# Storing the rows of x from SyncE's queue in place of GpSimd's, in an attention and two-stage expert kernel

## The chip, the cores and the metric

The kernel runs on one core of a Trainium2 chip. The metric is device time in microseconds. A core has five engines with instruction queues of their own: TensorE (PE; PEld is its weight load), VectorE (DVE), ScalarE (ACT), GpSimd (POOL) and SyncE (SP), which only issues transfers here. Transfers run on 16 DMA engines that all issuers share. Each engine takes its instructions strictly in order; waits between engines, and for transfers to land, are semaphores.

## The reference

Three stages follow one another: block attention, a layer of experts with one expert per token, and a second dense layer with a maximum of three products.

```python
# attention: B, H, S, D = 8, 8, 576, 64, in chunks of 64 keys
scores = scale * np.matmul(q_c, k_c.transpose(0, 1, 2, 4, 3))
attn = np.exp(scores - np.max(scores, axis=-1, keepdims=True))
attn = attn / (np.sum(attn, axis=-1, keepdims=True) + 1e-09)
out = np.matmul(attn, v_c)
x = out.transpose(0, 2, 1, 3).reshape(B * S, H * D)        # 4608 tokens x 512
# experts: a token with x @ w_skip > 0 goes to expert argmax(x @ w_gate)
h = np.maximum(xc[mask] @ w1[e], 0.0)                       # 512 -> 1024
y[mask] = gate_w[mask, None] * (h @ w2[e])                  # 1024 -> 512
out[do_compute] = xc + y
# second layer
h = np.maximum(np.maximum(x @ w1, x @ w2), x @ w3)          # 512 -> 768
return h @ w_out
```

## The kernel before

The 4608 tokens are 36 tiles of 128. A loop over t = 0 to 35 runs the attention as a pipeline: in step t the scores of tile t, the values and the scaling of tile t - 2, the transpose of x of that tile, and the logits of tile t - 3. Four tiles make a group g (nine groups). The rows of x of a group lie in one buffer `xg` of 128 partitions x 4 tiles x 520 floats; there are two such buffers, so group g + 2 writes where group g was. `scaled(t)` writes a tile's rows (L361, VectorE); at a group's first tile a memset on GpSimd fills the padding columns first (L357). `route(g)` and `gates(g)` choose the experts on VectorE; `gates(g)` writes one gate value per row (L432) and then calls `store_x(g)`, the function of this study, which copies the buffer to `x_dram`. Later the experts' rows are gathered from `x_dram` by indirect transfers on GpSimd.

GpSimd has further work in this loop: it copies halves of v across partitions (`cross`, L259), pairs the heads of q and k (`pair_heads`, `pair_big`, L233), rounds expert weights (L771), and sends each token's number to its slot in a table in DRAM (`send_id`, L524). SyncE loads q and k (L213, L222, L226), v (L252), expert weights (L100, L763), and reads the table of slots back (L540), once the sends have landed. Its loads of q, k and v run up to eight tiles ahead of their use.

What sets the order: on PE, DVE, ACT and POOL the program's order inside `by_hand` is kept as it is written. On SyncE a scheduler with a timeline of its own decides it. Every transfer of a queue takes one of eight semaphores in turn (DMAHW0 to 7 for SyncE), and waits until the one that had it before has landed.

```python
parts = [bpool.tile([P, GT, XW], F32, tag="xg", name=f"xg{g}")]   # two buffers
...
nc.vector.reciprocal(part[:, :, DM], sm[:, i * n:i * n + n])
store_x(g)
```

Of the kernel before, what the change touches and what calls it, by code (L numbers as in the profile page):

```python
# [19 lines left out]
P = 128  # L20
# [20 lines left out]
def kernel(  # L41
# [15 lines left out]
    nc = tc.nc  # L57
# [5 lines left out]
    x_dram = dram.tile([N + 1, XW], F32, name="x_dram")  # L63
# [356 lines left out]
    def gates(g):  # L420
        parts, nt = groups[g][0], SIZES[g]
        T = slice(0, nt)
        ex, m8, comp = routing[g]
        oh, eo = picks[g]
        sm = apool.tile([P, GT], F32, tag="rsm", name=f"rsm_{g}", bufs=1)
        nc.vector.reduce_sum(sm[:, T], ex[:, T], axis=AX)
        nc.vector.tensor_scalar(eo[:, T], m8[:, T], float(-COLS), float(E * COLS + P * SLOTS), op0=ALU.mult, op1=ALU.add)
        nc.vector.tensor_scalar_add(sm[:, T], sm[:, T], 1e-9)
        nc.vector.scalar_tensor_tensor(eo[:, T], comp[:, T], float(-P * SLOTS), eo[:, T], op0=ALU.mult, op1=ALU.add)
        for i, part in enumerate(parts):  # L430
            n = part.shape[1]
            nc.vector.reciprocal(part[:, :, DM], sm[:, i * n:i * n + n])  # L432
        store_x(g)
        before, after = run[g % 2], run[(g + 1) % 2]
        got = apool.tile([P, E], F32, tag="rgot", name=f"rgot_{g}", bufs=1)
        nc.vector.reduce_sum(got, oh[:, T].rearrange("p t e -> p e t"), axis=AX)
        nc.vector.tensor_tensor(after, before, got, op=ALU.add)
# [104 lines left out]
    def store_x(g):  # L542
        r = START[g] * P
        for part in groups[g][0]:
            n = part.shape[1] * P
            nc.gpsimd.dma_start(x_dram[r:r + n, :].rearrange("(t p) c -> p t c", p=P), part)
            r += n

    def apart(ins, own, other):
# [785 lines left out]
    for b, (r0, n) in enumerate(BLOCKS):  # L1335
# [31 lines left out]
        for half in range(2):  # L1367
            for i in range(n // P):
# [11 lines left out]
                r = r0 + half * n + i * P  # L1380
# [34 lines left out]
```

## Time and profile before

| | |
|---|---|
| median of three timed runs | 1050.54 us (1046.76 to 1053.8) |
| the profiled execution | 1043.47 us |
| its span in the trace | 1041.8 us |
| TensorE busy | 999.0 us |
| VectorE busy | 575.4 us |
| ScalarE busy | 420.2 us |
| GpSimd busy | 315.6 us |
| the nine stores of x | 1040.0 KB each |

All times inside the trace count from the start of the span. The span is one profiled execution, some 1.7 us shorter than the time of that execution, and that execution was a little faster than the timed ones. "Idle before" is the time in which an engine did nothing before an instruction, with what ended it; a row of SyncE is the issuing of a transfer, not the transfer.

### The profile page before, as it was taken

Reading aid. Unit: us, or ns where it says so; the run is one execution under the profiler, and the core shown is the slowest. Engines: PE = TensorE matmul, PEld = TensorE weight load, DVE = VectorE, ACT = ScalarE, POOL = GpSimd, SP = SyncE. Lnnn points to the kernel's source line nnn. Section 1 sums busy time; section 2 is a strip of 40 time slices with the busy share of each in tenths; the row PEclk is TensorE's granted clock in tenths of the full one; section 3 lists DMA queues with packets and bytes.
Section 4 is the critical chain, followed back from the end, with each engine's and each line's share of the span. In section 5 each row is a group of like instructions: output and inputs, shape, how many; then the busy total and the mean of one; then the engine's idle time right before and its main releaser. Section 6 shows DMA issues by size and latency. Waiting matters only on the chain.

```text
span 1041.8 us, 19679 instructions
## 1 busy us (share of the span) xinstructions
PE 999.0 (96%) x7569; PEld 855.2 (82%) x7569; DVE 575.4 (55%) x1100; ACT 420.2 (40%) x762; POOL 315.6 (30%) x359
## 2 busy tenths in 40 slices
PE   8998999998989999899999999999999999999996
PEld 7988988888777888787878887788888888878995
DVE  4676888688273795655898524343344424434241
ACT  5876874455251554424443422223222322223230
POOL 3665867512120343105321502213012311103010
PEclk9998999999999999999999999999999999999999
DMA  9999973877281795659995446645566356674771
GB/s 235 295 307 293 238 237 111 260 248 272 87 284 62 250 329 200 234 188 349 339 319 169 149 142 185 192 132 172 162 193 190 103 168 200 185 222 156 224 232 40
DMA packets 198258, 217.44 MB, mean 209 GB/s; under 512 B 47195, under 2 KB 162027, under 8 KB 198144
## 3 DMA queue, kind: packets, MB, share of 16 engines
q1 hardware_dynamic: 185328, 176.27, 55.7%
q0 software_dynamic: 10224, 31.40, 8.7%
q10 hardware_dynamic: 2592, 8.26, 2.1%
q8 instruction: 70, 1.15, 0.5%
q14 instruction: 44, 0.36, 0.1%
HBM read 175.30 MB, written 41.98 MB: 209 GB/s over the span
## 4 chain that ended last, share of the span: by engine, by line
PE 51%; DMA 3%; DVE 2%; issue 0%; ACT 0%; SPq 0%; DVEq 0%; ACTq 0%
PE f_a L663 6%; PE f_a L665 6%; PE f_a L664 6%; PE o L663 5%; PE o L665 5%; PE o L664 5%; PE f_d L663 3%; PE f_d L665 3%; PE f_d L664 3%; DMA ws<-m_sums 2%; PE f_b L663 2%; PE f_b L665 2%; PE f_b L664 2%; PE trf L1124 1%; DMA x<-x_dram 1%; PE h L663 0%
## 5 line engine op out<-in xcount | busy, mean ns | idle before, releaser
L94 POOL TENSOR_TENSOR fh<-best,fh 128x512 fp32r<-128x512 f32 (+1 forms) x60 | 75.2, 1260 | 358.1 <-ACT fh L93 271.1
L663 PE MATMUL f_a<-x_t,ws 128*128 128x512 f32 (+1 forms) x270 | 100.3, 372 | 0.8 <-DVE best L1298 0.8
L665 PE MATMUL f_a<-x_t,ws 128*128 128x512 f32 (+1 forms) x270 | 99.6, 369 | 0.0
L664 PE MATMUL f_a<-x_t,ws 128*128 128x512 f32 (+1 forms) x270 | 99.5, 369 | 0.0
L664 PE MATMUL o<-wlo_m,fh 128*128 128x512 f32 x216 | 84.6, 392 | 0.0
L663 PE MATMUL o<-whi_m,fh 128*128 128x512 f32 x216 | 84.5, 392 | 0.0
L665 PE MATMUL o<-whi_m,fh 128*128 128x512 f32 x216 | 83.4, 393 | 0.0
L943 POOL DMA_INDIRECT x_dram<-xg,ids_sb x20 | 30.0, 1501 | 172.5 <-DVE xg L941 81.0
L93 ACT CAST whi_e<-raw_e 128x1024 fp32r<-128x1024 f32 x56 | 58.2, 1051 | 58.8 <-DMA raw_e<-in_moe_w_dram 39.0
L663 PE MATMUL h<-xhi,whi_e 128*128 128x256 f32 x256 | 73.5, 287 | 7.9 <-PEq L1240 2.8
L94 DVE TENSOR_TENSOR wlo_e<-raw_e,whi_e 128x1024 fp32r<-128x1024 f32 x56 | 68.0, 1222 | 20.6 <-ACT whi_e L93 20.2
L663 PE MATMUL y<-whi_e,hhi 128*128 128x512 f32 x184 | 74.0, 403 | 0.9 <-ACT hhi L1012 0.9
L93 ACT CAST fh<-best 128x512 fp32r<-128x512 f32 (+1 forms) x60 | 34.5, 579 | 95.0 <-DVE best L1300 58.3
L664 PE MATMUL h<-xlo,whi_e 128*128 128x256 f32 x256 | 72.5, 283 | 0.2 <-issue 0.2
L665 PE MATMUL y<-whi_e,hlo 128*128 128x512 f32 x184 | 72.5, 397 | 0.2
L665 PE MATMUL h<-xhi,wlo_e 128*128 128x256 f32 x256 | 72.5, 283 | 0.0
L664 PE MATMUL y<-wlo_e,hhi 128*128 128x512 f32 x184 | 72.2, 393 | 0.0
L1130 POOL TENSOR_TENSOR x_t<-t,x_t 128x512 fp32r<-128x512 f32 (+1 forms) x40 | 46.1, 1182 | 50.9 <-ACT x_t L1129 50.9
L1303 ACT COPY p<-f_a 128x512 f32<-128x512 f32 (+1 forms) x45 | 24.3, 543 | 87.0 <-PE f_a L665 86.8
L663 PEld LDWEIGHTS f_a<-x_t,ws 128*128 128x128 f32 x270 | 51.0, 189 | 9.9 <-DVE best L1298 1.6
L665 PEld LDWEIGHTS f_a<-x_t,ws 128*128 128x128 f32 x270 | 50.9, 189 | 8.6
L663 PEld LDWEIGHTS h<-xhi,whi_e 128*128 128x128 f32 x256 | 49.2, 192 | 10.7 <-issue 9.3
(242 smaller groups left out, 2604.8 us busy)
## 6 DMA issues: line engine op xcount, KB each, us to landing
ws<-m_sums SPq DMA_DIRECT2D x135, 512.0 KB
raw_e<-in_moe_w_dram SPq DMA_DIRECT2D x64, 512.0 KB
ws<-m_sums SPq DMA_DIRECT2D x45, 256.0 KB
x_dram<-xg POOLq DMA_DIRECT2D x9, 1040.0 KB, 6.5
x<-x_dram SPq DMA_DIRECT2D x36, 256.0 KB
v_all<-in_v_dram SPq DMA_DIRECT2D x32, 256.0 KB
out_dram<-os SPq DMA_DIRECT2D x32, 256.0 KB
m_sums<-n_raw ACTq DMA_DIRECT2D x18, 448.0 KB
```

The costliest lines, as they stand in the source:

```text
L93: nc.scalar.copy(hi, src),
L94: eng.tensor_tensor(lo, src, hi.bitcast(F32), op=ALU.subtract),
L663: nc.tensor.matmul(acc, ahi, bhi, start=first, stop=False, skip_group_check=onto)
L664: nc.tensor.matmul(acc, ahi, blo, start=False, stop=False, skip_group_check=onto)
L665: return nc.tensor.matmul(acc, alo, bhi, start=False, stop=last, skip_group_check=onto)
L943: ins = nc.gpsimd.indirect_dma_start(out=x_dram[:, :], out_offset=bass.IndirectOffsetOnAxis(ap=ids, axis=0), in_=xg, in_offset=None, bound ...
L1124: nc.tensor.transpose(tr[:, i * P:(i + 1) * P], row[:, c * P:(c + 1) * P], ident)
L1130: eng.tensor_tensor(lo, src, hi.bitcast(F32), op=ALU.subtract)
L1303: nc.scalar.copy(p1, acc_a)
```

## The change

A group's store is issued by SyncE and no longer by GpSimd. Size, source, destination and the work on the four computing engines stay.

```diff
     def store_x(g):
         r = START[g] * P
         for part in groups[g][0]:
             n = part.shape[1] * P
-            nc.gpsimd.dma_start(x_dram[r:r + n, :].rearrange("(t p) c -> p t c", p=P), part)
+            nc.sync.dma_start(x_dram[r:r + n, :].rearrange("(t p) c -> p t c", p=P), part)
             r += n
```

The order on PE, DVE and ACT is the same. On SyncE, at about t = 10 to 13 of the loop, the rows before were these; `qt` and `kt` are buffers of q and k, `v_all` of v, and in brackets is what a row waits for.

```order
L222 DMA qt_927<-in_q_dram 128x4x256 [waits DMAHW3_49,Pool_49]
L222 DMA kt_928<-in_k_dram 128x4x256 [waits DMAHW4_49,Pool_49]
L252 DMA v_all_139<-in_v_dram 128x8x64 [waits DMAHW5_49,PE_49,Activation_49]
L222 DMA qt_1121<-in_q_dram 128x4x256 [waits DMAHW6_49,Pool_49]
L222 DMA kt_1122<-in_k_dram 128x4x256 [waits DMAHW7_49,Pool_49]
L252 DMA v_all_140<-in_v_dram 128x8x64 [waits DMAHW0_49,PE_49,Activation_49]
L252 DMA v_all_141<-in_v_dram 128x8x64 [waits PE_49,DMAHW1_49,Activation_49,Pool_49]
```

Now, in the same place, with `xg_374`, the buffer of group 0:

```order
L222 DMA qt_927<-in_q_dram 128x4x256 [waits DMAHW3_49,Pool_49]
L222 DMA kt_928<-in_k_dram 128x4x256 [waits DMAHW4_49,Pool_49]
L252 DMA v_all_139<-in_v_dram 128x8x64 [waits DMAHW5_49,PE_49,Activation_49]
L546 DMA x_dram<-xg_374 128x4x520 [waits DMAHW6_49,DVE_49]
L222 DMA qt_1121<-in_q_dram 128x4x256 [waits DMAHW7_49,Pool_49]
L222 DMA kt_1122<-in_k_dram 128x4x256 [waits DMAHW0_49,Pool_49]
L252 DMA v_all_140<-in_v_dram 128x8x64 [waits DMAHW1_49,PE_49,Activation_49]
L252 DMA v_all_141<-in_v_dram 128x8x64 [waits PE_49,DMAHW2_49,Activation_49,Pool_49]
```

The store of group 0 stands between two loads and waits for VectorE's gates; the loads behind it wait until it is issued.

On VectorE the order is the same, and the rows around the first scaling of group 2 (`xg_1148`, the buffer that `xg_374` had) are now these; before, the same row waited for DMASW5, a semaphore of GpSimd's queue.

```order
L359 TENSOR_SCALAR sm_1151<-xp_1131 128x8 [waits PE_49]
L360 RECIPROCAL sm_1151<-sm_1151 128x8 [waits DVE_49]
L361 TENSOR_TENSOR xg_1148<-xp_1131,sm_1151 128x2x4x64 [waits DMAHW6_49,DVE_49,Pool_49]
L313 TENSOR_REDUCE mx_1173<-sc_1156 128x8 [waits PE_49]
L315 TENSOR_TENSOR ex_1175<-sc_1156,mx_1173 128x2x4x64 [waits DVE_49,Activation_49]
L401 TENSOR_REDUCE rmx_1204<-lg_735 128x4 [waits Activation_49]
```

The wait for the buffer goes from GpSimd's semaphore to SyncE's, and the maximum and the subtraction of the tile stand behind it.

On SyncE, near the end of the loop, the difference is this; `ids_121` and `ids_sb` are the slot lists, and 2776, 3181 and 3550 are the buffers of groups 6, 7 and 8.

```order
 L540 DMA ids_121<-ids_dram_67 128x3
 L540 DMA ids_sb<-ids_dram_67 128x288
+L546 DMA x_dram<-xg_2776 128x4x520
+L546 DMA x_dram<-xg_3181 128x4x520
 L540 DMA ids_120<-ids_dram_68 128x1
+L546 DMA x_dram<-xg_3550 128x4x520
 L616 DMA n_raw_4513<-in_moe_w_dram 128x2x512
 L616 DMA n_raw_4791<-in_moe_w_dram 128x2x512
```

The stores of groups 6 and 7 come behind two loads of slot lists that wait for GpSimd's sends, and that of group 8 behind a third.

## Rows read from the trace of the kernel before

**Rows 1.** The page: busy time of each engine, and the stores among the issues.

```profile
PE 999.0 (96%) x7569; PEld 855.2 (82%) x7569; DVE 575.4 (55%) x1100; ACT 420.2 (40%) x762; POOL 315.6 (30%) x359
...
x_dram<-xg POOLq DMA_DIRECT2D x9, 1040.0 KB, 6.5
```

**Rows 2.** Waits of TensorE, 40 to 190 us: total us, times, longest us.

```profile
PE sc L306 <- issue: 6.0, 4, 2.5
PE lp L385 <- ACT xt L379: 1.0, 1, 1.0
PE xp L345 <- issue: 0.9, 2, 0.5
PE lp L385 <- issue: 0.5, 1, 0.5
PE rk L458 <- DVE roh L415: 0.4, 1, 0.4
PE trx L374 <- DVE xg L361: 0.2, 1, 0.2
```

**Rows 3.** Stretches: us, PE, PEld, DVE, ACT, POOL busy, then PEclk, DMA share, GB/s.

```profile
40.00:56.00 16.00, 14.71 (x309) 13.92 (x309) 9.99 (x33) 11.55 (x26) 11.02 (x23) 1.00 1.03 300
56.00:70.00 14.00, 14.00 (x324) 13.17 (x324) 12.12 (x37) 11.79 (x27) 8.80 (x14) 1.00 1.09 312
...
92.00:99.00 7.00, 7.00 (x92) 6.55 (x90) 4.55 (x15) 3.58 (x9) 1.41 (x3) 0.51 1.02 247
99.00:103.00 4.00, 4.00 (x93) 3.84 (x93) 1.92 (x11) 2.94 (x8) 2.87 (x5) 1.00 0.70 216
```

**Rows 4.** Timeline of GpSimd: start, us, instruction, idle before and its releaser.

```profile
44.70 0.78 POOL L546 DMA_DIRECT2D x_dram<-xg  x1
...
55.13 0.12 POOL L357 MEMSET xg<- 128x28 f32 x1 [0.26 <-DMA x_dram<-xg]
...
62.44 0.82 POOL L546 DMA_DIRECT2D x_dram<-xg  x1 [3.93 <-DVE run L437]
...
148.83 0.81 POOL L546 DMA_DIRECT2D x_dram<-xg  x1 [4.77 <-DVE run L437]
```

**Rows 5.** Timeline of SyncE, 53 to 76 us.

```profile
57.56 1.06 SPq L252 DMA_DIRECT2D v_all<-in_v_dram  x1
...
72.26 1.64 SPq L100 DMA_DIRECT2D raw_e<-in_moe_w_dram  x1
```

**Rows 6.** Timeline of VectorE: first scalings of groups 2, 3 and 8.

```profile
55.20 0.69 DVE L361 TENSOR_TENSOR xg<-xp,sm 128x512 f32<-128x512 f32 x1 [0.54 <-DMA x_dram<-xg]
...
56.60 0.69 DVE L315 TENSOR_TENSOR ex<-sc,mx 128x512 f32<-128x512 f32 x1
...
70.78 0.69 DVE L361 TENSOR_TENSOR xg<-xp,sm 128x512 f32<-128x512 f32 x1 [0.18 <-DMA x_dram<-xg]
...
158.20 0.69 DVE L361 TENSOR_TENSOR xg<-xp,sm 128x512 f32<-128x512 f32 x1
```

**Rows 7.** Timeline of TensorE, around 57 and 91 us.

```profile
56.82 0.60 PE L374 MATMUL trx<-ident,xg 128*128 128x128 f32 x4
...
58.70 0.66 PE L329 MATMUL trp<-ident,ex 128*128 128x128 f32 x4
...
90.88 0.21 PE L306 MATMUL sc<-kT,qT 64*64 64x64 f32 x1 [2.50 <-issue]
```

**Rows 8.** Line L546, the stores: duration ns min/median/max; issue to landing.

```profile
L546 POOL DMA_DIRECT2D x_dram<-xg x9: 778/802/821, 44.7 to 177.0; - x9
...
DMA to landing us min/median/max: 4.9/6.5/8.2
```

**Rows 9.** Waits of GpSimd, 40 to 190 us: total us, times, longest.

```profile
POOL x_dram L546 <- DVE run L437: 20.1, 6, 4.8
```

**Rows 10.** Timeline of ScalarE: the exponential of the tile around 57 us.

```profile
57.63 0.63 ACT L322 ACTIVATE ex<-ex 128x512 f32<-128x512 f32 x1
```

**Rows 11.** Timeline of SyncE: the second load of a slot list.

```profile
156.48 0.42 SPq L540 DMA_DIRECT2D ids_sb<-ids_dram  x1
```

## The prediction

> **What bounds the kernel now.** I read the page's busy times first: TensorE is busy 999.0 of 1041.8 us [rows 1], so a microsecond counts if TensorE stands for it. The nine stores belong to the first 180 us (attention and routing), so the next view is TensorE's waits there [rows 2]. No row names GpSimd, SyncE or a load. The 7.4 us of three groups (6.0 + 0.9 + 0.5) have no cause that the profile shows, 1.4 us are waits for ScalarE and for VectorE's choice of expert, and 0.2 us is a transpose of x that waited for VectorE's xg. That last one looks small and is the one to follow. The table of stretches comes third: from 40 to 70 us the 16 DMA engines are taken all the time (share 1.03 and 1.09 at 300 and 312 GB/s) [rows 3]. So in this stage SyncE's queue is a line at a full counter: it runs as fast as the engines move bytes, and its place in the program says little about its place in time. Then I set the same group of rows side by side on GpSimd, SyncE and VectorE.
>
> A store of group g frees one of two xg buffers, and group g + 2 writes that buffer first in GpSimd's memset (L357) and VectorE's scaling (L361). Group 0's store is issued by GpSimd at 44.70, and the memset at 55.13 and the scaling at 55.20 both were waiting for it to land, for 0.26 and 0.54 us [rows 4, 6]. So already now this store takes 10.4 us and has no slack. Group 1's store, issued at 62.44, again releases the scaling at 70.78 after a wait of 0.18 us [rows 4, 6].
>
> **What the change removes.** Nine issues at a median of 802 ns [rows 8] leave GpSimd, 7.2 us of its time, and with them the waits ahead of six of them, 20.1 us in all, in which GpSimd stood for VectorE's gates [rows 9]. What stood behind these waits on GpSimd were the sends of slots, the crossing copies of v and the pairing of q and k. TensorE waited for none of these in this stage [rows 2], so the gain on the path is 0. Its bounds: not below 0, and not above the 7.4 us without a cause, if those were GpSimd's after all. Nothing is saved on the DMA engines either: nine times 1040 KB [rows 1] move as before.
>
> **What it adds: group 0's store in SyncE's queue.** The order of the new program puts it right behind the load of v that stands, before, directly ahead of the loads of the twelfth pair of q and k. SyncE issues that v load at 57.56 and is through with it at 58.62 [rows 5], 14 us after GpSimd issued the store. So the store, ready at the same time as before, waits in line. It gets there a little sooner than 58.6, since its own bytes have not been moved ahead of it: 1040 KB are 1.065 MB, at some 306 GB/s (the mean of 300 and 312, [rows 3]) 3.5 us. That is 55.1 at the earliest, 58.6 at the latest. From issue to landing the stores take 4.9 / 6.5 / 8.2 us (least, median, most, [rows 8]). Group 0's own store took 10.4 us, but in that lies its wait beside SyncE's loads, which the later issue already counts here. I take the early issue and the median: 55.1 + 6.5 = 61.6. The ends are 60.0 (55.1 + 4.9) and 69.0 (58.6 + 10.4).
>
> The scaling that began at 55.20 then begins at 61.6: VectorE stands 6.4 us longer (4.8 to 13.8), and behind it in its order are the maximum and the subtraction of the current tile (the subtraction is over at 56.60 + 0.69 = 57.29 now, [rows 6]), the routing of group 1 and so on. TensorE's transposes of that x begin at 56.82 [rows 7], 0.93 us after the scaling's end (55.20 + 0.69 = 55.89). That is the slack; 5.5 us are left (3.9 to 12.9). The other way to TensorE is no longer: subtraction to 57.29, the exponential at 57.63 for 0.63 us [rows 10], the transposes of the exponentials at 58.70 [rows 7], again under a microsecond of slack, and in series with the first only beyond it. **5.5 us.**
>
> GpSimd stands at the same memset until 61.6, then has a send, a crossing copy and a pair to do, some 3 us; TensorE is behind by then too, and the wait for group 1's gates, which would have come next, is gone. 0.
>
> **The clock.** TensorE standing has a second price here. At 90.88 it had stood for 2.50 us [rows 7]; from 92 to 99 the granted clock is 0.51, the lower of its two levels (1.2 of 2.4 GHz), and 92 matmuls take 7.00 us where the next 93 take 4.00 [rows 3]: 3.0 us lost. A stand of 5.5 us should do the same; the bounds are 0 and, if the lower clock lasts twice as long, 6. **3.0 us.**
>
> **The other eight stores.** Group 1's stands behind the load of a first expert matrix: SyncE is through with that at 72.26 + 1.64 = 73.90 [rows 5], less 3.5 for its own bytes 70.4, plus 6.5 is 76.9. Its scaling, at 70.78 before, has slack 0.9 and is itself 5.5 us later, 77.2. A tie; I take 0, with a late end in the rivals. Later groups have the lead that the first stand gives to the queue, and the engines are less taken (share 0.70 from 99 to 103 us, [rows 3]). Group 6's store changes places most: it falls behind SyncE's two loads of slot lists, which wait for sends on GpSimd (issued at 156.48 now, [rows 11], against 148.83 for the store, [rows 4]). But those sends themselves stood behind GpSimd's store, which waited 4.77 us [rows 4]; without it they go out some 5 us sooner, so the store is issued near 152 and lands, with 4.9 to 6.5, at 157 to 158.5. The scaling that needs the buffer is at 158.20 [rows 6]. 0, at most 2. The last store is freed for the gather of the leftover rows; TensorE has other work there. 0.
>
> **The sum.** 5.5 + 3.0 = 8.5 us on the profiled execution: 1043.47 + 8.5 = 1052.0. The median of the three timed runs is 1050.54, 7.07 above that execution; the forecast is against the median: 1050.54 + 8.5 = **1059.0**. The sum's own range: 3.9 to 12.9 for the stand, 0 to 6 for the clock, hence 1054 to 1069 with not both at their upper ends.
>
> **The rivals.** *Paid back.* The stand happens, but while it lasts the DMA engines clear the line, and after it TensorE's idle times without a shown cause do not come back: they all fall where the engines are full, and the largest of them (2.50 us) brought the 3.0 us of clock. For it: rows 2 and 3 together. Against: nothing shows that they come from transfers. 8.5 less the 6.9 us in the groups of scores and values and less 3.0 is -1.4; with half of that coming back it is +3.5. So 1049 to 1054, I say 1051.
>
> *The queue makes no difference.* In the trace a store takes the same 16 engines whoever issues it, and SyncE's issues there last 1 to 3 us [rows 5]. If that time were only the engines' and the store went through with the loads around it, it would land by 56 and cost nothing: 1050.5. The Trainium skill, page "DMA: Bandwidth & Descriptors", section "Issuing engines are not separate DMA queues", gives this as a rule: all DMAs end on the same 16 engines and interleave, and spreading them over issuers saves only the issuing time. The trace agrees with the part on the engines and speaks against the rest, since the two queues stood 14 us apart at this point. The same page, section "Queues, rings and completion order", says that an engine takes turns between queues but consumes one queue in its order; that is the forecast's side.
>
> *Late again.* One more late store decides it: group 1's. If it is issued at 73.9 and lands after 8.2, at 82.1, its scaling is late by 82.1 - 70.78 - 0.9 = 10.4 us in place of 5.5, and the clock falls twice, 6.0: 1067. It decides from a landing later than 77.2, which is 0.3 us from my middle value. This is the case that ends slower.
>
> *GpSimd was in the way.* The stand doesn't come, and the 7.4 us and the 3.0 us of clock were GpSimd's lateness: 1050.5 - 10.4 = 1040. Against it: no row of TensorE's waits names GpSimd.
>
> **How the numbers follow.** Forecast 0.47, paid back 0.23, no difference 0.08, late again 0.17, GpSimd in the way 0.05. One per cent, about what a measurement here can tell from nothing, is 10.5 us: 1040 to 1061. Over 1061 lies a quarter of the forecast's own spread (0.12) and late again (0.17): 0.29. Under 1040 half of the last case, 0.03. Between them 0.68. The range 1047 to 1066 leaves out the last case and the upper part of late again with the forecast's far end, some 0.18.
>
> **What would show it.** In the trace after: SyncE's first L546 near 55 to 59 us and not near 45; VectorE's L361 of group 2's first tile waiting 4.8 to 13.8 us for the store; TensorE's L374 right behind it standing 4 to 13 us; a granted clock near 0.5 in the microseconds after that; GpSimd's waits of 20.1 us gone with no gain of TensorE. The next scalings (group 3, group 8) waiting under 2 us. I am wrong if SyncE reaches the store by 50 us, if VectorE's wait is long and TensorE's is not, or if the waits at groups 3 and 4 are as long as the first.

## The result, and the profile after

The change costs one per cent: a median of 1055.57 us against 1046.1 us for the kernel before on the same chip, with a ratio of 1.0103 [1.0082, 1.0123], which is 10.8 us (8.6 to 12.9); the two medians are 9.5 us apart. The forecast was 1059.0, within 1% and slower. Ratios, here and below, are of undisturbed runs alone (1046.41 to 1060.42 us for the changed kernel) and need not be the quotient of the two medians. The execution that was profiled took 1068.15 us, longer than any of these; so little more than its first 100 us is read here, and two further profiles of the changed kernel, with spans of 1056.4 and 1048.6 us, stand beside it in the experiments.

The page of the kernel after, busy times; to be held against [rows 1]:

```profile
PE 1009.7 (95%) x7569; PEld 864.4 (81%) x7569; DVE 573.2 (54%) x1100; ACT 421.0 (39%) x762; POOL 311.4 (29%) x350
```

GpSimd has lost nine instructions and 4.2 us of busy time, and TensorE gained nothing by it that its waits show. The waits of TensorE from 40 to 190 us (total us, times, longest), as in [rows 2]:

```profile
PE trx L374 <- DVE xg L361: 8.3, 1, 8.3
PE sc L306 <- issue: 6.5, 4, 2.2
PE lp L385 <- ACT xt L379: 1.0, 1, 1.0
PE xp L345 <- issue: 0.9, 1, 0.9
```

The row that was 0.2 us is now 8.3 us, in one piece; the idle time without a shown cause is what it was, and its largest piece is 2.2 us where it was 2.5. Where the 8.3 us come from is seen with the timelines of SyncE, VectorE, GpSimd and TensorE (start us, us, instruction, and in brackets the idle time before it with its releaser). First SyncE, 53 to 60 us, to be held against [rows 5]:

```profile
55.25 1.04 SPq L252 DMA_DIRECT2D v_all<-in_v_dram  x1
56.38 1.25 SPq L546 DMA_DIRECT2D x_dram<-xg  x1
57.73 1.31 SPq L222 DMA_DIRECT2D qt<-in_q_dram  x1
```

The store of group 0 is issued at 56.38, directly behind the v load that the order named, and 11.7 us later than GpSimd issued it (44.70, [rows 4]). VectorE, where group 2 writes the same buffer for the first time, to be held against [rows 6]:

```profile
64.44 0.69 DVE L361 TENSOR_TENSOR xg<-xp,sm 128x512 f32<-128x512 f32 x1 [9.83 <-DMA x_dram<-xg]
65.05 0.68 DVE L313 TENSOR_REDUCE mx<-sc 128x8 f32<-128x512 f32 x1
65.84 0.69 DVE L315 TENSOR_TENSOR ex<-sc,mx 128x512 f32<-128x512 f32 x1
```

It stood 9.83 us for the store where it had stood 0.54, and the maximum and the subtraction stood behind it. GpSimd's memset of the same buffer stood 10.49 us, against 0.26 in [rows 4]:

```profile
64.37 0.12 POOL L357 MEMSET xg<- 128x28 f32 x1 [10.49 <-DMA x_dram<-xg]
```

And TensorE's transposes of that x, at 56.82 before [rows 7]:

```profile
65.28 1.08 PE L374 MATMUL trx<-ident,xg 128*128 128x128 f32 x4 [8.35 <-DVE xg L361]
```

They are 8.46 us late, nearly all of it the stand of 8.35. The transposes of the next tile, first in the kernel before and then in the changed one:

```profile
60.91 0.60 PE L374 MATMUL trx<-ident,xg 128*128 128x128 f32 x4
```

```profile
71.39 0.60 PE L374 MATMUL trx<-ident,xg 128*128 128x128 f32 x4
```

What the stand does to the clock is read in the stretches (us, then PE, PEld, DVE, ACT, POOL busy, then PEclk, DMA share, GB/s):

```profile
57.00:64.00 7.00, 0.00 (x0) 0.00 (x0) 0.00 (x0) 0.56 (x1) 0.00 (x0) 0.71 1.04 334
64.00:71.00 7.00, 5.72 (x85) 5.30 (x86) 6.21 (x17) 2.67 (x6) 4.67 (x8) 0.55 1.06 262
71.00:78.00 7.00, 7.00 (x176) 6.65 (x175) 5.14 (x21) 5.53 (x13) 2.21 (x4) 1.00 1.11 330
...
100.00:107.00 7.00, 6.95 (x91) 6.36 (x91) 3.87 (x13) 3.55 (x8) 4.55 (x7) 0.57 0.71 214
```

For a whole stretch of 7 us TensorE does nothing while the DMA engines are full. The granted clock is at the lower of its two levels from 59.99 to 70.23 us, which is from 3 us into the stand to 5 us behind its end, and 85 matmuls are done in 5.72 busy us of one stretch where 176 are done in the 7.00 of the next. The transposes of the next tile are 10.48 us late, 2.0 us more than the first ones; those 2.0 us are what the clock cost. The last row shows that the fall of the clock behind the 2.2 us of idle time (it was 0.51 from 92 to 99 us, [rows 3]) came back as well.

### The profile page after: what moved, and what is told of

Same layout as the page of the kernel before. It is cut to its first block, busy times and chain, and to the rows that moved or that the text cites. A ratio compares the mean times of both kernels' runs of the same rounds, so it can differ in the third digit from the quotient of the medians.

```text
span 1066.4 us, 19683 instructions
## 1 busy us (share of the span) xinstructions
PE 1009.7 (95%) x7569; PEld 864.4 (81%) x7569; DVE 573.2 (54%) x1100; ACT 421.0 (39%) x762; POOL 311.4 (29%) x350
## 4 chain that ended last, share of the span: by engine, by line
PE 47%; DMA 5%; DVE 2%; issue 1%; ACT 0%; SPq 0%; DVEq 0%; ACTq 0%
PE f_a L663 6%; PE f_a L665 6%; PE f_a L664 6%; PE o L663 5%; PE o L664 5%; PE o L665 5%; PE f_d L663 3%; PE f_d L665 3%; PE f_d L664 3%; DMA ws<-m_sums 2%; DMA x<-x_dram 1%; PE f_b L663 1%; PE f_b L664 1%; PE f_b L665 1%; PE trf L1124 1%
## 5 line engine op out<-in xcount | busy, mean ns | idle before, releaser
L943 POOL DMA_INDIRECT x_dram<-xg,ids_sb x20 | 27.2, 1361 | 175.3 <-DVE xg L941 81.0
L663 PEld LDWEIGHTS f_a<-x_t,ws 128*128 128x128 f32 x270 | 50.9, 189 | 11.7 <-DVE best L1298 3.4
L663 PEld LDWEIGHTS h<-xhi,whi_e 128*128 128x128 f32 x256 | 49.7, 194 | 10.5 <-issue 9.3
```

The costliest lines, as they stand in the source:

```text
L663: nc.tensor.matmul(acc, ahi, bhi, start=first, stop=False, skip_group_check=onto)
L943: ins = nc.gpsimd.indirect_dma_start(out=x_dram[:, :], out_offset=bass.IndirectOffsetOnAxis(ap=ids, axis=0), in_=xg, in_offset=None, bound ...
```

## The experiments

The theory is called **place in line**: what counts is when group 0's store lands, and on SyncE's queue it stands behind loads whose issuing takes SyncE 1 to 5 us each while the DMA engines are full. Its rival is that **SyncE's queue costs by itself**, through each of nine stores or through the loads behind them. Each experiment is timed against the kernel before on the same chip; edits are shown against the kernel before, with `...` where lines are left out.

**Group 0's store alone on SyncE.**

```diff
-            nc.gpsimd.dma_start(x_dram[r:r + n, :].rearrange("(t p) c -> p t c", p=P), part)
+            (nc.sync if g == 0 else nc.gpsimd).dma_start(x_dram[r:r + n, :].rearrange("(t p) c -> p t c", p=P), part)
```

> Only group 0's store goes to SyncE; the other eight stay on GpSimd. Place in line (the store waits behind SyncE's loads, its buffer comes free late and VectorE and TensorE stand once): the whole loss is here, +8 to +12 us, with VectorE waiting 7 to 10 us at group 2's first scaling and TensorE standing 6 to 9 us. Cost per store (each store on SyncE's queue costs about the same, by its issue or by holding up loads): a ninth, +1 us.

1048.18 us against 1041.02, ratio 1.0068 [1.0032, 1.0104]: 7.1 us (3.3 to 10.8), far more than a ninth and just under the 8 to 12 expected. One store of nine gives the whole event; whether the other eight add a part of the full change's 1.0%, the overlapping intervals don't tell. VectorE's timeline, and the stretches that follow, of this kernel:

```profile
63.47 0.69 DVE L361 TENSOR_TENSOR xg<-xp,sm 128x512 f32<-128x512 f32 x1 [9.96 <-DMA x_dram<-xg]
```

```profile
60.00:67.00 7.00, 2.70 (x66) 2.40 (x68) 3.36 (x8) 1.33 (x3) 2.67 (x5) 0.50 1.17 308
67.00:74.00 7.00, 7.00 (x101) 6.78 (x101) 3.84 (x17) 3.44 (x7) 2.89 (x5) 0.52 1.05 273
74.00:81.00 7.00, 7.00 (x144) 6.53 (x138) 5.20 (x14) 5.35 (x12) 3.96 (x6) 1.00 1.06 348
```

The wait of 9.96 us is that of the full change (9.83), TensorE stands 8.48 us, and the clock is at half level from 60.05 to 73.70. TensorE's transposes are then 11.5 us later than in the first profile of before, and 8.6 us near 116 us: some of the event was given back.

**All but group 0's on SyncE.**

```diff
+            (nc.gpsimd if g == 0 else nc.sync).dma_start(x_dram[r:r + n, :].rearrange("(t p) c -> p t c", p=P), part)
```

> Only group 0's store stays on GpSimd, the other eight go to SyncE. Place in line: the wait moves to the next buffer. Group 1's store is issued by SyncE near 70 us and lands near 77, where group 3's first scaling is ready at 70.8: VectorE waits 4 to 8 us there, TensorE stands 3 to 7, with the clock +5 to +9 us. Cost per store: eight ninths, +8 to +9 us, without one long wait.

1054.34 us, ratio 1.0124 [1.0067, 1.018]. These 12.9 us (7.0 to 18.7) lie above what either theory expected (5 to 9 us), so the time does not tell them apart; the one long wait does. The wait at group 2 is gone, and one of the same kind stands one group later, since group 1's store is now the first of the nine on SyncE's queue. SyncE and VectorE of this kernel:

```profile
71.04 0.37 SPq L546 DMA_DIRECT2D x_dram<-xg  x1
```

```profile
80.14 0.69 DVE L361 TENSOR_TENSOR xg<-xp,sm 128x512 f32<-128x512 f32 x1 [8.79 <-DMA x_dram<-xg]
```

TensorE stood 7.3 us there, with the clock at half level from 76.9 for 13.7 us. In the kernel before, the same scaling waited 0.18 us for GpSimd's store, issued at 62.44 [rows 4, 6].

**Groups 0 to 2 on GpSimd, the rest on SyncE.**

```diff
+            (nc.gpsimd if g < 3 else nc.sync).dma_start(x_dram[r:r + n, :].rearrange("(t p) c -> p t c", p=P), part)
```

> Groups 0, 1 and 2 stay on GpSimd, the other six go to SyncE. Place in line: nothing is lost, -2 to +2 us, and no scaling waits over 2 us for its buffer, since the later buffers are needed after SyncE's queue has caught up. Cost per store: six ninths, +6 to +7 us.

1053.5 us, ratio 1.0112 [1.0055, 1.0169], 11.7 us (5.7 to 17.6): the expectation of place in line fell, because it had taken the queue to be free of its lag by then. It isn't. The 6 to 7 us of a cost per store lie inside this interval; against it stands that the trace has one long wait. SyncE and VectorE of this kernel, at the store of group 3 and the scaling that waits for it:

```profile
107.82 4.46 SPq L226 DMA_DIRECT2D kt<-in_k_dram  x3
112.38 0.55 SPq L546 DMA_DIRECT2D x_dram<-xg  x1
```

```profile
120.22 0.69 DVE L361 TENSOR_TENSOR xg<-xp,sm 128x512 f32<-128x512 f32 x1 [5.58 <-DMA x_dram<-xg]
```

The store stands behind three pieces of k that take 4.46 us to issue, TensorE stands 4.1 us, and the clock is at half level from 120.5 to 130.8. Its transposes are 4.7 us later than in the first profile of before ahead of this event and 13.1 us behind it, so the event is 8.4 us; the 4.7 us come from an idle stretch of 2.81 us that ends at 42.9, which the other profiles have smaller or not at all, and 10.2 us of half clock around it. In the full change the store of group 3 was not waited for. So the theory needs an amendment: the first of the nine on SyncE's queue is late, whichever group's it is, as long as the queue lags; its stand holds the computing engines back, not the loads, and the later stores profit from that lead. That fits the costs of one, six, eight and nine stores, 0.7, 1.1, 1.2 and 1.0%, which do not grow with their number; the lead itself was not varied.

**All nine on ScalarE.**

```diff
+            nc.scalar.dma_start(x_dram[r:r + n, :].rearrange("(t p) c -> p t c", p=P), part)
```

> All nine stores go to ScalarE's queue, which has no loads in this stage. Place in line: the store is issued near 44 us, as on GpSimd, lands before 56, and no scaling waits over 2 us; -1 to +4 us, the plus for ScalarE's issues (nine of 0.4 to 1.3 us) and its waits for the gates. If it is the path of the hardware queues itself that loses, by slower writes or worse mixing with the loads, the loss stays: +8 to +12 us.

1055.51 us, ratio 1.0111 [1.0046, 1.0175]: a miss again, and not for a late landing. ScalarE's timeline, its store and the copy behind it:

```profile
54.08 0.39 ACTq L546 DMA_DIRECT2D x_dram<-xg  x1
54.57 0.58 ACT L332 COPY aT<-trp 128x512 f32<-128x512 f32 x1 [9.03 <-DMA v_all<-in_v_dram]
```

ScalarE had come to the store at 45.5 us and stood 9.03 us for a load of v that SyncE had issued at 46.29. In the order the store waits for DMAHW7, one of the eight semaphores that transfers of SyncE and ScalarE take in one common turn here (not SyncE's alone), and the transfer that had it before was that load, the last part of which landed at 54.01. TensorE stood 7.5 us for ScalarE's copy. SyncE's lag reached the store through the semaphore. This run says nothing against a ScalarE queue with semaphores of its own, which was not tried.

**All nine on SyncE, but the loads behind them.** The loads of q, k and v from step 5 on are ordered three steps later, and behind the last store issued; nothing is left out.

```diff
+            link["store"] = nc.sync.dma_start(x_dram[r:r + n, :].rearrange("(t p) c -> p t c", p=P), part)
...
+        while held_loads and held_loads[0][0] <= t:
+            _, load, n = held_loads.pop(0)
+            with tc.issue_after(link["store"].ins) if "store" in link else nullcontext():
+                load(n)
...
-            load_qk(u + 6)
+            load_later(t, load_qk, u + 6)
...
-                load_v(t - 2 + NV)
+                load_later(t, load_v, t - 2 + NV)
```

> All nine stores on SyncE's queue, as in the change, but the loads of q, k and v from step 5 on are ordered three steps later and behind the last store issued, so that group 0's store stands behind a load that was issued near 45 us before. Place in line: the store is issued at 44 to 48 us, lands by 55, the first scaling of group 2 waits for it under 2 us, and the loss of 1.0% goes: -2 to +2 us. SyncE's queue costs by itself, wherever in it the store stands: the store still lands 8 us or more late, and the loss stays at +8 to +12 us. A third way: the loads, three steps later, come late themselves; then the control run with the same loads and GpSimd's stores shows the same loss.

The control has the same edit with the stores on GpSimd.

> Control: the stores stay on GpSimd's queue, and the loads of q, k and v are ordered three steps later as in the run with SyncE's stores. Place in line: no wait over 1 us at the first scalings, and a time within 3 us of the kernel before; if loads come late by it, the extra time is to be taken off the other run's.

1051.97 us against 1047.6 with SyncE's stores, ratio 1.0042 [1.0013, 1.0072]; 1050.12 us with GpSimd's, ratio 1.0024 [0.9988, 1.006]. The 4.4 us of the first are more than the 2 expected, and the control says why: the later loads seem to cost 2.5 us themselves, and with that taken off the stores on SyncE cost 0.18%, some 2 us, where they cost 1.0% behind the loads; the two intervals overlap, so this rest may be nothing. SyncE, VectorE and TensorE of the kernel with SyncE's stores:

```profile
45.01 0.46 SPq L546 DMA_DIRECT2D x_dram<-xg  x1
```

```profile
55.19 0.69 DVE L361 TENSOR_TENSOR xg<-xp,sm 128x512 f32<-128x512 f32 x1 [1.11 <-DMA x_dram<-xg]
```

```profile
56.21 0.60 PE L374 MATMUL trx<-ident,xg 128*128 128x128 f32 x4
```

Issued at 45.01, the store frees its buffer at 55.19; GpSimd's, issued at 44.70, freed it at 55.20 [rows 4, 6]. On SyncE's queue, in the right place, the transfer is as good as before, and TensorE doesn't stand.

**Late without SyncE.** The kernel before, with one step moved: GpSimd issues group 0's store later in the loop.

```diff
-        store_x(g)
+        if g:
+            store_x(g)
...
+    LATE_STORE = 9
...
+        if t == LATE_STORE:
+            store_x(0)
```

> The kernel before with one step moved: GpSimd issues group 0's store at step 9 of the loop, near 52 us, and not near 45 us; SyncE's queue holds no store. Place in line (only the landing time counts, whichever queue brings it): it lands near 58.5 to 60, VectorE's first scaling of group 2 waits 3.4 to 7 us, TensorE stands 2.5 to 6 us, and with 0 to 3 us of clock the time is +2.5 to +9 us. SyncE's queue costs by itself: no loss, within 2 us of the kernel before.

1056.88 us against 1047.6, ratio 1.0101 [1.005, 1.0152]: the whole loss, with no store on SyncE. GpSimd and VectorE of this kernel (one line further down in its file):

```profile
52.34 0.81 POOL L547 DMA_DIRECT2D x_dram<-xg  x1
...
61.02 0.12 POOL L357 MEMSET xg<- 128x28 f32 x1 [4.84 <-DMA x_dram<-xg]
```

```profile
61.09 0.69 DVE L361 TENSOR_TENSOR xg<-xp,sm 128x512 f32<-128x512 f32 x1 [5.76 <-DMA x_dram<-xg]
```

TensorE, in the same kernel:

```profile
61.92 1.09 PE L374 MATMUL trx<-ident,xg 128*128 128x128 f32 x4 [4.30 <-DVE xg L361]
```

It stood 4.30 us, and then from 64 to 71 us it did 93 matmuls at a granted clock of 0.50. Its transposes were 5.1 us late at the first tile, 8.2 at the next and 9.2 at the one after, with half clock from 61.28 to 71.52: 4.1 us of clock. The wait and the stand lie within what was expected; the clock is above the 3 us expected, and with it the time (9.3 us between the medians, 10.6 by the ratio).

**Further profiles of both kernels.** The shift of the first profile grew behind 100 us, from 10 to 25 us at its end; is that the change?

> The changed kernel once more beside the three others on the same chip. Place in line: +8 to +12 us, with the stand of TensorE near 57 to 66 us and the half clock around it, no other first scaling waiting over 2 us, and no further growth of the shift behind 100 us, if the growth in the first profile was that execution's own. Late again at later stores: a second wait of 3 us or more at groups 3 to 8.

> The changed kernel, profiled a third time. The wait of the first scaling of group 2 comes again, 8 to 10 us, with TensorE standing 7 to 8.5 us and a stretch of half clock around it; no other first scaling waits over 2 us for a store. Half clock from 140 to 190 us comes or not, as it falls.

> The kernel before, profiled once more. In the first profile of it no stretch from 140 to 190 us was at half clock, while the changed kernel's has two there (6.8 us each from 153.0 and 176.9), and its shift grows from 8 us at 140 us to 16 us at 190 us. If these stretches are each execution's own, they show up here too, in one profile of two at least, and the first scaling of group 2 again waits under 1 us. If they follow from the change (late again, later on), TensorE's clock stays whole from 140 to 190 us in both.

> As the first of the two: half clock somewhere from 140 to 190 us in at least one of the two if it is each execution's own; in neither if it follows from the change.

The changed kernel once more: 1056.85 us against 1047.6, ratio 1.0093 [1.006, 1.0126]. VectorE in its profile, and in the third one:

```profile
63.15 0.69 DVE L361 TENSOR_TENSOR xg<-xp,sm 128x512 f32<-128x512 f32 x1 [8.49 <-DMA x_dram<-xg]
```

```profile
64.68 0.69 DVE L361 TENSOR_TENSOR xg<-xp,sm 128x512 f32<-128x512 f32 x1 [7.98 <-DMA x_dram<-xg]
```

The event comes each time, with TensorE standing 7.03 and 6.52 us (in the third profile wait and stand fall just short of the 8 and 7 us expected), and no other first scaling waits for a store. What comes later varies: against expectation the shift of the second profile grew as well, from 7.7 us near 140 us to 16.4 at the last tile, while that of the third stayed at 5.8 to 7.1 there. Half clock from 140 to 190 us was there in all three profiles of the changed kernel (10.2, 13.7 and 3.4 us of it) and in the two new ones of the kernel before as well (6.8 us from 162.9, 3.4 us from 167.4), so it is no mark of the change, though the first profile of before had none; whether the change makes it longer, three profiles don't tell. The single times were 1050.28 us for the changed kernel and 1040.04, 1043.58 and 1041.78 for the kernel before on that chip. The span of the third profile, 1048.6 us, is 8.0 above the mean of the three of the kernel before (1041.8, 1038.3 and 1041.8).

## Why the prediction was right

**The place in line.** SyncE was to reach the store at 55.1 to 58.6. It did so at 56.38, 55.02 and 56.54 in three profiles (the second 0.1 early), with the v load ahead of it sooner than before. Moving the loads behind the store took the wait away, and moving GpSimd's own store brought it back, so the landing time is shown to be the cause.

**The landing** was the term of the sum that was too small. The 6.5 us were taken for the median of all nine stores [rows 8]; from issue to the released scaling it was 8.1 us in each of the three profiles (64.44 - 56.38, 63.15 - 55.02, 64.68 - 56.54). Asked store by store, the trace of the kernel before gives a landing for only three of the nine: 8.2 us for group 1's, issued at 62.44, and 6.5 and 4.9 us for those issued at 148.83 and 165.56, where the DMA share is 0.55 (145 to 160 us) and 0.33 (160 to 175 us). So the figure came from a stretch where the engines are half free. The right one stood in the rows: group 1's store, from the full stretch, released its scaling 8.3 us after its issue (70.78 - 62.44, [rows 4, 6]).

**The stand of TensorE** was to be 5.5 us (3.9 to 12.9) and was 8.35, 7.03 and 6.52. In the first profile the difference of 2.85 us is the landing (8.06 - 6.5 = 1.56) and the issue at 56.38 in place of 55.1 (1.28); the slack of 0.93 and the chain from VectorE's wait to TensorE's held. In the third profile TensorE itself came to the stand 2.1 us later (59.00 for 56.94), for reasons of its own.

**The clock** was to cost 3.0 us (0 to 6). The shift grew by 2.0, 1.4 and 1.7 us from the first tile behind the stand to the next, and by 4.0 us over two tiles where group 0 alone was moved. A part of the half clock falls into the stand and costs nothing there; the prediction had priced it whole, after the fall at 92 us, which came behind the idle time and not in it.

**The other eight stores** were to cost 0, and no first scaling waited for one. The reason given for the later groups, that the first stand gives the queue the lead, is borne out: without that stand group 1's store is late, and without stores 0 to 2 on the queue group 3's is; that it is the stand which gives it is argued from these, not tried by itself. The second half of the reason, that the engines are less taken there, isn't: group 3's was late at a DMA share of 0.84 (110 to 120 us).

**GpSimd's freed time** shows no gain. Its waits of 20.1 us for the gates [rows 9] are gone; 10.49 us came back at the memset.

**The sum** was 8.5 us. The rows of the first profile give 8.46 + 2.0 = 10.5 us, the stand and the clock of the second and third 7.03 + 1.4 = 8.4 and 6.52 + 1.7 = 8.2; the timed difference is 9.5 us between the medians and 10.8 (8.6 to 12.9) by the ratio. That it came so near is in part luck: the landing was too short by 1.6 us and the clock too dear by 1.0 to 1.6. The forecast missed 1055.57 by 3.5 us because its base, the three runs shown of before (1050.54), lay 4.4 us above the median of all 22 (1046.1), while the sum was 1.0 too low by the medians and 2.3 by the ratio. (The range's 1069 is the sum with both terms at their upper ends, not short of that.)

**The rivals.** *The queue makes no difference* fell: the stand came, at a price of 1%. The Trainium skill, page "DMA: Bandwidth & Descriptors", section "Issuing engines are not separate DMA queues", says that whichever engine starts a transfer, it ends on the same 16 DMA engines, and that several issuers save only the time of issuing. The runs agree with it where the place in time is the same (10.2 us from issue to the freed buffer on SyncE's queue, 10.5 on GpSimd's) and differ on what an issuer is worth: at this point another issuer was worth 11.7 us of place. *Late again* did not come at group 1's store; its mechanism is real, as the run with groups 1 to 8 shows. *GpSimd was in the way* fell with the sum. *Paid back* is half open. In the first profile the largest group of idle times without a shown cause came again at the same size (6.5 for 6.0 us), with the fall of the clock, against it. For it: the pause near 97 us was 1.40 us in the second profile and 0.85 and 0.78 us in the runs with groups 1 to 8 on SyncE and with ScalarE, where the three profiles of before have 2.2 to 2.5 (near 88 us), and the clock stayed whole behind it, where these three have 3.4 to 6.8 us of half clock. So some executions get a part of the event back; in the second and third profiles of the changed kernel the shift against the first of before shrank from 9.6 and 10.5 us near 70 us to 7.0 and 6.2 near 115 us, but the two new profiles of the kernel before were themselves 1.5 and 2.8 us ahead of the first there. The timed loss of the full change, about as large as the event itself, leaves little room for it on the average.

## What to carry to other kernels

Before a store moves to another queue, look at how far that queue lags behind its place in the program: issues of 1 to 5 us, as SyncE's were here at a DMA share of 1.0 to 1.1, hold up whatever is put behind them. A store that frees a buffer belongs on a queue that is idle when the data are ready, or ahead of the loads that run far in front of their use. Price its landing by transfers from the same stretch, not by the median of all, and look for the first late buffer: here it was paid once, and the later stores were not waited for.

## What the runs showed of the hardware

- TensorE stood 4.1 to 8.5 us, and the granted clock was at its lower level for 6.8 to 13.7 us in one piece around that stand. What the clock cost went with the part of it behind the stand's end, not with the length of the stand: 3.7 to 5.0 us of half clock behind the end cost 1.4 to 2.0 us (the three profiles of the change, stands of 6.5 to 8.4 us), and 9.4 to 9.7 us cost 4.0 to 4.1 us (group 0 alone, groups 1 to 8, groups 3 to 8, and GpSimd late, stands of 8.48, 7.33, 4.11 and 4.30 us).
- A transfer issued by ScalarE waited 9.03 us for one of SyncE's, through the semaphore that they take in a common turn in this program. ScalarE's queue, which has no loads in this stage, was not a free one while these turns are shared.
- From issue to the freed buffer the same 1040 KB of group 0 took 8.1 us behind the loads on SyncE's queue, 8.8 us late on GpSimd's, and 10.2 to 10.5 us ahead of the loads, in a stretch where the DMA share was about 1.0; group 1's and group 3's on SyncE's queue took 9.1 and 7.8 us. What sets the difference was not tried.
- In the kernel before the issuing of a transfer on SyncE's queue took from 0.4 to 4.8 us between 40 and 80 us, where the DMA share was 1.0 to 1.1; in the changed kernel that of the 1040 KB took 1.25 us at 56.38 and 0.38 us at 72.72. What makes single ones short in this stretch stays open.
- An idle time of TensorE of 1.4 to 2.5 us without a shown cause, near 88 to 100 us, comes in every one of the three profiles of either kernel. What it waits for stays open.
